# Loads in 2 KB rows, matmul turns, permuted units and new slots in a recurrence-plus-maxout kernel

## Chip, cores, metric

The kernel runs on one core of a Trainium2 chip. The metric is the device time of one execution in microseconds. A profiled execution took some 1.75 us more than the span that its trace shows (402.07 over 400.3). Ratios are computed from fast runs alone: the mean time of one kernel's fast runs over that of the other's in the same rounds, so they are not quite the ratio of the medians quoted.

## The reference

Inputs are float32: x and f_logit of 4 x 6144 x 256, a bound per channel, and three weight matrices.

```python
sig = 1.0 / (1.0 + np.exp(-f_logit))
f = lower_bound + (1.0 - lower_bound) * sig
h = 0
for t in range(S):                       # per batch and channel
    h = f[:, t] * h + (1.0 - f[:, t]) * x[:, t]
    y[:, t] = h
h1, h2 = y @ w1, y @ w2                  # 24576 tokens, 256 -> 1024
out = np.maximum(h1, h2) @ w_out         # 1024 -> 256, float32
```

## The kernel before

The kernel writes max(h1, h2) as h1 + relu(h2 - h1). The engines are called PE (TensorE), ACT (ScalarE), DVE (VectorE), POOL (GpSimd) and SP (SyncE, which issues DMAs). A block of 512 tokens needs "hidden" matmuls with the difference w2 - w1, relus, and a projection with w_out plus a linear part, w1 @ w_out, that is computed once. There are 48 blocks. The scan needs channels on partitions, so tokens must be turned (transposed). Blocks 0 to 3 (the opening) are loaded in float32 and turned on TensorE. Later blocks go in chunks of two through a casting DMA to a scratch tensor and a transposing DMA. The opening's work is a list of items (`PLAN`): G gate (u = sigmoid(-f_logit)), V drive (v = u x), TU and TV turns of u and v, F forget (f from u), S scan, RW rounding of w1 to bf16, D difference of weights, SC its scaling, TW turn of w1, KW its copy, W linear weights, H hidden, R relu, P projection step, warm idle matmuls that only keep TensorE busy; a letter after the dot names the engine (a ACT, v DVE, p POOL).

```python
def load(j, s, q0, q1, eng=nc.sync):                  # 256 KB, rows of 1 KB
    src = (f_logit, x)[s]
    eng.dma_start(out=ins[j][s][:, q0:q1, :],
        in_=src[0, j*TB + q0*P : j*TB + q1*P, :].rearrange("(q p) d -> p q d", p=P))

def turn_pe(j, s, x):
    dst = (uT, vT)[s][j, x] = ps_d.tile([P, KC, HB], BF16, name="dT")   # in PSUM
    src = (us, vs)[s][j]
    for q in range(2):
        for h in range(KC):
            nc.tensor.transpose(dst[:, h, q*P:(q+1)*P],
                                src[:, 2*x+q, h*P:(h+1)*P], ident_b[:])
# [...]
w1n = wpool.tile([P, KC, DFF], FP32)                  # all of w1, four loads of 256 KB
# [...]
def round_w1(k, eng):                                 # one quarter, after its load
    cols = slice(k*QF, (k+1)*QF)
    cast_on(eng, w1b[:, :, cols], w1n[:, :, cols])
# [...]
def diff(k, h, eng):
    cols = slice(k*QF, (k+1)*QF)
    eng.tensor_tensor(out=wdf[:, h, cols], in0=w2n[:, h, cols],
                      in1=w1n[:, h, cols], op=ALU.subtract)
# [...]
for j in range(3, NBLK + 1):                          # the steady loop
    for fc in range(FC):                              # a slot: 0.978 us
        if j < NBLK:
            hidden(j, fc)                             # two 128x512 matmuls and a relu on ACT
        project(j - 1, fc)                            # five 128x256 matmuls
        # [...] stores
        if (j, fc) in gate_of: ...                    # gate, drive, forget, scan of a later block
        if (j, fc) in turn_of: ...                    # transposing DMA of a chunk, cast of the next
```

## Time and profile before

| | before |
|---|---|
| median of 3 runs | 401.4 us (400.9 to 403.14) |
| span of the profiled run | 400.3 us |
| first hidden matmul | 10.18 us |
| first matmul of the loop | 36.08 us |
| start of the last projection | 391.91 us |
| 45 blocks at the loop's pace | 351.9 us |

The page's slices say how busy an engine is. The busy time by stretch says where TensorE is not full, and the timeline says what it waits for there. The prediction below shows those lines and the budget that comes out of them.

### The profile page before, as it was taken

What the parts mean: (1) busy time and instruction counts of PE and PEld (TensorE: products, weight loads), DVE (VectorE), ACT (ScalarE), POOL (GpSimd) and SP (SyncE); (2) the same over time, 40 slices, a digit from 0 to 9 for tenths busy, and PEclk for the clock granted to TensorE, in tenths of its full rate; (3) what the DMA queues carried; (4) which work ended last, traced back from release to release, by engine and by line L of the source; (5) the groups of instructions that cost most, each with busy time, mean ns of one, the idle gap of its engine ahead of it and who ended that gap; (6) DMA issues with size and microseconds to landing.
All of it is one profiled execution on the core that took longest, in us unless ns stands there. A gap on an engine that the chain in (4) does not pass through costs nothing.

```text
span 400.3 us, 7223 instructions
## 1 busy us (share of the span) xinstructions
PE 390.6 (98%) x2854; PEld 276.1 (69%) x2854; DVE 251.5 (63%) x365; ACT 273.8 (68%) x452; POOL 42.3 (11%) x83
## 2 busy tenths in 40 slices
PE   8999999999999999999999999999999999999996
PEld 3887677666777677766776677667776777667764
DVE  4976775738576567657755765676576567657622
ACT  5777675766766676677667667766766776676661
POOL 2511010110111010110110110110201101100000
PEclk9999999999999999999999999999999999999999
DMA  8989996989999999999999999998999999895122
GB/s 259 349 213 202 216 212 145 195 192 218 233 219 218 205 181 219 200 192 218 195 189 222 195 200 212 184 234 186 180 213 209 196 223 194 191 215 146 52 99 87
DMA packets 125110, 79.12 MB, mean 198 GB/s; under 512 B 94226, under 2 KB 101652, under 8 KB 125076
## 3 DMA queue, kind: packets, MB, share of 16 engines
q1 hardware_dynamic: 112836, 55.33, 54.4%
q0 software_dynamic: 11968, 23.07, 35.5%
q8 instruction: 22, 0.36, 0.4%
q10 hardware_dynamic: 272, 0.26, 0.2%
q14 instruction: 12, 0.10, 0.1%
HBM read 53.48 MB, written 48.23 MB: 254 GB/s over the span
## 4 chain that ended last, share of the span: by engine, by line
PE 85%; DMA 7%; DVE 4%; ACT 1%; SPq 1%; issue 1%; DVEq 0%; ACTq 0%
PE psO L263 47%; PE dT L243 35%; DVE y L147 2%; DMA fn<-in_f_logit_dram 2%; PE dT L223 2%; DMA won<-in_moe_w_out_dram 1%; DMA w2n<-in_moe_w_dram 1%; DMA fT<-fs 1%; DMA xT<-xs 1%; ACT u L195 1%; DVE v L199 1%; SPq L178 1%; DVE ff L136 1%; PE dT L124 0%; DVE osb L312 0%
## 5 line engine op out<-in xcount | busy, mean ns | idle before, releaser
L238 ACT ACTIVATE rt<-dT 128x512 bf16<-128x512 f32 x379 | 221.9, 596 | 105.9 <-PE dT L243 103.0
L263 PE MATMUL psO<-wob,rt 128*128 128x256 bf16 x1536 | 231.5, 273 | 2.2 <-ACT rt L238 1.7
L263 PEld LDWEIGHTS <-rt 128*128 128x128 bf16 x1536 | 149.9, 98 | 98.1 <-ACT rt L238 2.5
L243 PE MATMUL dT<-y,wd 128*128 128x512 bf16 x720 | 214.3, 379 | 0.9 <-DVE y L147 0.9
L147 DVE TENSOR_TENSOR_SCAN y<-ff,y,v 128x512 bf16<-128x512 bf16 x82 | 105.3, 1284 | 2.9
L199 DVE TENSOR_TENSOR v<-u,xT 128x1024 bf16<-128x1024 bf16 x44 | 30.4, 692 | 102.3 <-ACT u L195 86.6
L312 DVE COPY osb<-psO 128x512 f32<-128x512 f32 x92 | 62.1, 679 | 28.6 <-PE psO L263 28.6
L243 PEld LDWEIGHTS <-wd 128*128 128x128 bf16 x720 | 70.5, 98 | 8.2
L263 PE MATMUL psO<-w,y 128*128 128x256 bf16 x384 | 72.6, 273 | 0.0
L195 ACT ACTIVATE u<-fT 128x1024 bf16<-128x1024 bf16 x44 | 46.2, 1049 | 4.2 <-DMA fT<-fs 4.2
L184 POOL CAST held<-fT 128x1 f32<-128x1 bf16 x21 | 10.1, 479 | 288.6 <-DMA fT<-fs 288.6
L263 PEld LDWEIGHTS <-y 128*128 128x128 bf16 x384 | 37.5, 98 | 4.4
L136 DVE TENSOR_SCALAR ff<-u,nom 128x512 bf16<-128x512 bf16 x88 | 29.8, 338 | 0.0
L223 PE MATMUL dT<-y,wd 128*128 128x256 bf16 x96 | 14.7, 273 | 0.0
L168 POOL DMA_DIRECT2D fs<-in_f_logit_dram x22 | 12.3, 558 | 2.8 <-issue 2.6
L168 POOL DMA_DIRECT2D xs<-in_x_dram x22 | 12.1, 550 | 0.0
L147 DVE TENSOR_TENSOR_SCAN y<-nff,y,dT 128x256 bf16<-128x256 bf16 x14 | 9.7, 734 | 2.1 <-PE dT L124 1.8
L223 PEld LDWEIGHTS <-wd 128*128 128x128 bf16 x96 | 9.1, 98 | 1.4 <-issue 0.2
L111 DVE TENSOR_TENSOR vn<-un,xn 128x512 bf16<-128x512 bf16 x8 | 6.0, 755 | 5.2 <-ACT un L106 3.3
L428 PE MATMUL psO<-warm 128*128 128x512 bf16 x21 | 7.6, 494 | 1.2 <-DVE warm L556 1.2
L106 ACT ACTIVATE un<-fn 128x512 bf16<-128x512 f32 x8 | 5.0, 628 | 4.5 <-DMA fn<-in_f_logit_dram 4.5
L147 DVE TENSOR_TENSOR_SCAN y<-ff,v 128x512 bf16<-128x512 bf16 x6 | 7.3, 1225 | 0.2
(41 smaller groups left out, 54.7 us busy)
## 6 DMA issues: line engine op xcount, KB each, us to landing
out_dram<-osb SPq DMA_DIRECT2D x95, 256.0 KB, 2.8
fs<-in_f_logit_dram POOLq DMA_DIRECT2D x22, 512.0 KB, 6.1
xs<-in_x_dram POOLq DMA_DIRECT2D x22, 512.0 KB, 9.1
fn<-in_f_logit_dram SPq DMA_DIRECT2D x8, 256.0 KB, 7.3
xn<-in_x_dram SPq DMA_DIRECT2D x7, 256.0 KB, 6.7
w1n<-in_moe_w_dram SPq DMA_DIRECT2D x4, 256.0 KB, 5.4
w2n<-in_moe_w_dram SPq DMA_DIRECT2D x4, 256.0 KB, 5.6
won<-in_moe_w_out_dram SPq DMA_DIRECT2D x4, 256.0 KB, 6.0
```

The costliest lines, as they stand in the source:

```text
L136: nc.vector.tensor_scalar(out=o, in0=i, scalar1=nom[:, h : h + 1], scalar2=1.0, op0=ALU.mult, op1=ALU.add)
L147: nc.vector.tensor_tensor_scan(out=ys[j][:, h, t0:t1], data0=ffs[j][:, h, t0:t1], data1=v, initial=initial, op0=ALU.mult, op1=ALU.add,)
L168: nc.gpsimd.dma_start(out=spare[c % NS, name][:], in_=src[b, k * TB : (k + CB) * TB, :], max_dma_last_dim=4096,)
L184: nc.gpsimd.tensor_copy(out=held[:], in_=turned[c, 0][:, KC - 1, last : last + 1])
L195: nc.scalar.activation(out=us[j][:], in_=part(j, 0), func=AF.Sigmoid, scale=-1.0)
L199: nc.vector.tensor_tensor(out=vs[j][:], in0=us[j][:], in1=part(j, 1), op=ALU.mult)
L223: nc.tensor.matmul(dts[j, fc][:, tok], lhsT=wd[:, kc, unit(fc)], rhs=ys[j][:, kc, tok], start=(first and kc == 0), stop=(not first and kc ...
L238: nc.scalar.activation(out=rt[:], in_=dts[j, fc][:], func=AF.Relu)
L243: nc.tensor.matmul(dts[j, fc][:], lhsT=wd[:, kc, unit(fc)], rhs=ys[j][:, kc, :], start=(kc == 0), stop=(kc == KC - 1),)
L263: nc.tensor.matmul(ps, lhsT=lhsT, rhs=rhs, start=start, stop=stop, skip_group_check=True)
L312: nc.vector.tensor_copy(out=osbs[j, g][:], in_=pos[j, g, 0][:])
L428: nc.tensor.matmul(idle[:].rearrange("p r d -> p (r d)"), lhsT=warm[:, 0:P], rhs=warm[:], start=True, stop=True,)
```

## The change

The intent: larger DMA rows for quicker loads, with the turns adapted to the new layout; an order of the opening made for the new loads; and loop slots that turn chunks and gate blocks earlier, so that no gate waits on a late chunk.

```diff
-        in_=src[0, j*TB + q0*P : ...].rearrange("(q p) d -> p q d", p=P)
+        in_=src[0, t0 : t0 + HB, :].rearrange("(p r) d -> p r d", r=2)     # two tokens a partition

-        dst = ps_d.tile([P, KC, HB], BF16, name="dT")
-                nc.tensor.transpose(dst[:, h, q*P:(q+1)*P], src[...], ident_b[:])
+        dst = ps_d.tile([P, KC, HB], FP32, name="dT")
+                nc.tensor.matmul(dst[:, h, r:HB:2], lhsT=src[...], rhs=ident_b[:], ...)

-            in_=moe_w_out[...].rearrange("(q p) c -> p q c", p=P)
+            in_=moe_w_out[...].rearrange("(p r) c -> p r c", r=2)           # permutes the units

-        cast_on(eng, w1b[:, :, cols], w1n[:, :, cols])
+        cast_on(eng, w1b[:, :, cols].rearrange("p h (r n) -> p h r n", r=2),
+                     w1n[:, :, cols].rearrange("p h (n r) -> p h r n", r=2))
 # [...] scale(): the same stepped view of wdf

-    f0a x0a f0b w13 w23 x0b w12 w22 wo3 w11 w21 w10 wo2 w20 f1a x1a wo1 f1b wo0 x1b
+    f0a x0a f0b x0b w1h w2h f1a wo0 w12 wo1 w22 w13 w23 x1a f1b wo2 x1b wo3 f2a f2b
 # [...] w1h, w2h: the first halves in one load each; PLAN in another order; every load but the
 # bound's on SP's queue (two x loads were on ACT's); hidden matmuls of block 2's end not in halves

-    turn_of = {(4, 1): 1, (6, 0): 2}
-    turn_of |= {(NP + c*CB - 3, 5): c for c in range(3, NCH)}
-    gate_of = {(3, 3): 4, (4, 0): 5, (5, 0): 6, (5, 5): 7, (6, 6): 8, (7, 3): 9}
+    turn_of = {(3, 5): 1, (5, 2): 2, (7, 0): 3}
+    turn_of |= {divmod(FC*(NP + c*CB - 3) - 3, FC): c for c in range(4, NCH)}
+    gate_of = {(3, 1): 4, (3, 6): 5, (4, 5): 6, (5, 3): 7, (6, 3): 8, (7, 1): 9}
 # [...] later gates one slot earlier; eight output buffers in place of six
```

More of the change, by code (lines that the diff above doesn't have):

```diff
@@ L60 @@
     rpool = ctx.enter_context(tc.tile_pool(name="rpool", bufs=3 * FC))
-    opool = ctx.enter_context(tc.tile_pool(name="opool", bufs=6))
+    opool = ctx.enter_context(tc.tile_pool(name="opool", bufs=8))
     lastpool = ctx.enter_context(tc.tile_pool(name="last", bufs=2))
@@ L94, in alloc_in, with load @@
         ys[j] = ypool.tile([P, KC, TB], BF16, name="y")
-    def load(j, s, q0, q1, eng=nc.sync):
+    def load(j, s, half):
         src = (f_logit, x)[s]
-        eng.dma_start(
-            out=ins[j][s][:, q0:q1, :],
-            in_=src[0, j * TB + q0 * P : j * TB + q1 * P, :].rearrange(
-                "(q p) d -> p q d", p=P
-            ),
+        t0 = j * TB + half * HB
+        nc.sync.dma_start(
+            out=ins[j][s][:, 2 * half : 2 * half + 2, :],
+            in_=src[0, t0 : t0 + HB, :].rearrange("(p r) d -> p r d", r=2),
         )
@@ L118, in turn_pe @@
     def turn_pe(j, s, x):
-        dst = (uT, vT)[s][j, x] = ps_d.tile([P, KC, HB], BF16, name="dT")
+        dst = (uT, vT)[s][j, x] = ps_d.tile([P, KC, HB], FP32, name="dT")
         src = (us, vs)[s][j]
-        for q in range(2):
+        for r in range(2):
             for h in range(KC):
-                nc.tensor.transpose(
-                    dst[:, h, q * P : (q + 1) * P],
-                    src[:, 2 * x + q, h * P : (h + 1) * P],
-                    ident_b[:],
+                nc.tensor.matmul(
+                    dst[:, h, r:HB:2],
+                    lhsT=src[:, 2 * x + r, h * P : (h + 1) * P],
+                    rhs=ident_b[:],
+                    start=(r == 0 and h == 0),
+                    stop=(r == 1 and h == KC - 1),
+                    skip_group_check=True,
                 )
@@ L238, in relu, with hidden_whole @@
             nc.scalar.activation(out=rt[:], in_=dts[j, fc][:], func=AF.Relu)
-    def hidden(j, fc):
+    def hidden_whole(j, fc):
         dts[j, fc] = ps_d.tile([P, TB], FP32, name="dT")
@@ L249, in hidden @@
             )
+    def hidden(j, fc):
+        hidden_whole(j, fc)
         relu(j, fc)
@@ L335, with weight_load @@
     QF = DFF // 4
-    def weight_load(k, w, src):
-        cols = slice(k * QF, (k + 1) * QF)
+    def weight_load(c0, c1, w, src):
         nc.sync.dma_start(
-            out=w[:, :, cols], in_=src[:, cols].rearrange("(h p) f -> p h f", p=P)
+            out=w[:, :, c0:c1], in_=src[:, c0:c1].rearrange("(h p) f -> p h f", p=P)
         )
@@ L345, in wout_load @@
             out=won[:, 2 * k : 2 * k + 2, :],
-            in_=moe_w_out[k * QF : (k + 1) * QF, :].rearrange("(q p) c -> p q c", p=P),
+            in_=moe_w_out[k * QF : (k + 1) * QF, :].rearrange("(p r) c -> p r c", r=2),
         )
@@ L356, in round_w1 @@
         cols = slice(k * QF, (k + 1) * QF)
-        cast_on(eng, w1b[:, :, cols], w1n[:, :, cols])
+        cast_on(
+            eng,
+            w1b[:, :, cols].rearrange("p h (r n) -> p h r n", r=2),
+            w1n[:, :, cols].rearrange("p h (n r) -> p h r n", r=2),
+        )
     pts = {}
@@ L380, in scale @@
         cols = slice(k * QF, (k + 1) * QF)
-        o, i, m = wd[:, h, cols], wdf[:, h, cols], om[:, h : h + 1]
+        o = wd[:, h, cols].rearrange("p (r n) -> p r n", r=2)
+        i = wdf[:, h, cols].rearrange("p (n r) -> p r n", r=2)
+        m = om[:, h : h + 1]
         if on_dve:
@@ L440 @@
     LOADS = """
-    f0a x0a f0b w13 w23 x0b w12 w22 wo3 w11 w21 w10 wo2 w20 f1a x1a wo1 f1b wo0 x1b
-    f2a x3b f3a x2a f2b x2b f3b x3a
+    f0a x0a f0b x0b w1h w2h f1a wo0 w12 wo1 w22 w13 w23 x1a f1b wo2 x1b wo3 f2a f2b
+    x2a x3b x2b f3b x3a f3a
     """
     PLAN = """
-    warm1 keeps_T G0a RW3.p V0a keeps TU0a D30.p F0a1.v G0b warm1 TV0a warm3 TU0b
-    F0a0.a S0a1 F0b0.a warm1 TW3 S0a0 F0b1.a KW3.a V0b SC30.a D31.p RW2.v D20.p
-    warm5 TV0b S0b0 D21.p D11.p S0b1 TW2 KW2.v SC31.a H07a SC21.v H06a RO3.a warm3
@@ L448 @@
-    H07b H06b SC20.a R07.a W133 H05a D10.v H05b R06.a RW0.a H04b SC10.v P071 SC11.v
-    H04a RW1.p P060 P061 R05.v D00.v H02b RO2.p TW0 R04.a H02a R02.a G1a D01.p TW1
-    RO1.p P040 H03b KW0.v KW1.a SC00.v P051 SC01.v H03a V1a R03.a W132 P070 TU1a
-    P041 H01b H00b H01a TV1a G1b F1a1.v H00a P030 P020 P031 R00.a RO0.p W131 TU1b
-    P021 F1a0.v S1a1 W130 R01.a P050 F1b0.a S1a0 G2a P010 KL1.a V1b TV1b KL0.a
-    F1b1.v P000 TU2a H11a H14a H16a S1b1 G3a P001 S1b0 P011 L01 F2a1.a H11b V2a H14b
@@ L454 @@
-    L00 F2a0.v H17a G2b O01.a R14.v TV2a L11 R11.a H16b L10 TU2b S2a0 R16.a G3b P140
-    H17b S2a1 H12a H12b P141 F2b1.v P111 R17.a H13b V2b H13a H15a R12.a F2b0.v H15b
-    TV2b P170 TU3b CA H10b H10a R15.a R13.v P110 F3b1.a TU3a R10.a F3b0.a S2b1 P121
-    P130 S2b0 V3a P151 H21a H21b F3a1.a P161 H26b H26a R21.a TV3a P100 V3b H24a
-    F3a0.v R26.a P131 S3a1 H24b H27b P171 H22b TV3b R24.a H27a P101 O00.a S3a0 S3b1
-    P150 R27.a H22a P160 H23a R22.a S3b0 H25b H25a H20b H23b H20a R25.a R23.v R20.v
@@ L460 @@
-    P120 O11.v O10.a
+    G0a RW0.p warm1 keeps_T TU0a keeps V0a F0a1.v D00.p D10.p warm2 TV0a G0b S0a1
+    warm3 TU0b V0b F0a0.a F0b0.a F0b1.a RW1.a S0a0 warm2 TV0b D11.p S0b1 warm3 TW0
+    RW2.p TW1 D01.v KW0.a SC00.a G1a SC01.v warm6 H00a S0b0 RO0.v H01a SC10.v H00b
+    TU1a R00.a SC11.v D21.p H01b KW1.a W130 P001 RW3.p H03b P000 D30.p F1a0.v RO1.v
+    R01.a D31.p D20.v H02a H02b H03a W131 TW2 P011 P010 SC21.v F1a1.a SC20.v R02.a
+    KW2.v TW3 H04a H04b RO2.p R03.a SC30.a V1a P021 KW3.v H05b SC31.v P020 G1b P030
@@ new lines @@
+    RO3.p P031 TV1a H05a TU1b R04.a H07a R05.a S1a0 F1b1.a H07b V1b H06b H06a P040
+    CA P041 S1a1 P050 TV1b F1b0.a S1b0 R06.a W132 R07.a H10a G2a H12a P051 W133 H16a
+    S1b1 P061 KL1.v H13a H12b KL0.v H10b H16b P070 V2a R12.v P071 G2b R10.a L01 V2b
+    TU2a H15b H13b P121 F2a0.v H15a R16.a TU2b TV2a O01.a R13.a F2b1.a L10 H11a
+    R15.a F2b0.a F2a1.v P100 S2a1 L11 TV2b H17a G3a P130 S2a0 H11b P161 S2b0 H17b
+    S2b1 H14b TU3a P060 H14a R11.a F3a1.v R17.a P150 P110 P120 H24 F3a0.v H21 V3a
@@ L461, with load_item @@
+    G3b P170 R14.a R24.a H23 R21.a TU3b V3b F3b0.a R23.v TV3a P140 H20 TV3b S3a1
+    F3b1.v P131 R20.a H27 P160 L00 H22 R27.a S3a0 P151 H26 H25 O10.a S3b1 R22.a P141
+    P171 P111 P101 S3b0 R26.a O00.v O11.v R25.a
     """
     engines = {"a": nc.scalar, "v": nc.vector, "p": nc.gpsimd}
-    def load_item(name, eng=nc.sync):
-        if name[0] == "w":
-            k = int(name[2])
-            if name[1] == "o":
-                wout_load(k)
-            elif name[1] == "1":
-                weight_load(k, w1n, moe_w1)
-            else:
-                weight_load(k, w2n, moe_w2)
-        else:
-            half = 2 * "ab".index(name[2])
-            load(int(name[1]), "fx".index(name[0]), half, half + 2, eng)
+    def load_item(name):
+        if name[:2] == "wo":
+            wout_load(int(name[2]))
+        elif name[0] == "w":
+            w, src = ((w1n, moe_w1), (w2n, moe_w2))[int(name[1]) - 1]
+            k = name[2]
+            weight_load(*((0, HF) if k == "h" else (int(k) * QF, (int(k) + 1) * QF)), w, src)
+        else:
+            load(int(name[1]), "fx".index(name[0]), "ab".index(name[2]))
@@ L523, in issue @@
         elif kind == "H":
-            hidden_half(*arg)
+            (hidden_half if len(arg) == 3 else hidden_whole)(*arg)
         elif kind == "R":
@@ L535, in issue @@
         elif kind == "CA":
-            nc.gpsimd.tensor_copy(out=held[:], in_=ins[2][0][:, 3, D - 1 : D])
+            nc.gpsimd.tensor_copy(out=held[:], in_=ins[2][1][:, 3, D - 1 : D])
             cast(0)
@@ L541, in issue @@
             raise ValueError(item)
-    turn_of = {(4, 1): 1, (6, 0): 2}
-    turn_of |= {(NP + c * CB - 3, 5): c for c in range(3, NCH)}
-    gate_of = {(3, 3): 4, (4, 0): 5, (5, 0): 6, (5, 5): 7, (6, 6): 8, (7, 3): 9}
-    gate_of |= {(b - 2, 5): b for b in range(10, NBLK)}
+    turn_of = {(3, 5): 1, (5, 2): 2, (7, 0): 3}
+    turn_of |= {divmod(FC * (NP + c * CB - 3) - 3, FC): c for c in range(4, NCH)}
+    gate_of = {(3, 1): 4, (3, 6): 5, (4, 5): 6, (5, 3): 7, (6, 3): 8, (7, 1): 9}
+    gate_of |= {(b - 2, 4): b for b in range(10, NBLK)}
     with tc.manual_schedule():
@@ L551 @@
             alloc_in(j)
-        for k, name in enumerate(LOADS.split()):
-            load_item(name, nc.scalar if k in (1, 3) else nc.sync)
-            if k == 0:
-                nc.sync.dma_start(out=lbr[:], in_=lower_bound.rearrange("(h p) -> h p", p=P))
+        nc.scalar.dma_start(out=lbr[:], in_=lower_bound.rearrange("(h p) -> h p", p=P))
+        for name in LOADS.split():
+            load_item(name)
         nc.vector.memset(warm[:], 0.0)
```

## The prediction

> **What bounds the kernel now.** I read the 40 slices first, then the busy time by stretch, then the timeline of PE where a stretch was not full, then the DMA view. On the page, PE is busy in almost every slice, at full clock:
>
> ```profile
> PE   8999999999999999999999999999999999999996
> PEclk9999999999999999999999999999999999999999
> ```
>
> A busy PE is not always a PE at its pace, so I split the span at the first hidden matmul (10.18 us), at the first matmul of the steady loop (36.08), at 100, and at the start of the last projection (about 392). Columns: busy time of PE, PEld, DVE, ACT, POOL with counts, clock, DMA share, GB/s.
>
> ```profile
> 10.18:36.08 25.90, 25.07 (x255) 22.03 (x253) 21.14 (x40) 20.05 (x38) 7.05 (x12) 1.00 1.03 255
> 36.08:100.00 63.92, 60.84 (x431) 41.73 (x429) 40.93 (x58) 42.78 (x70) 4.91 (x11) 1.00 0.93 199
> 100.00:392.00 292.00, 292.00 (x2094) 204.69 (x2092) 182.59 (x254) 205.64 (x335) 27.26 (x51) 1.00 0.91 193
> ```
>
> From 100 to 392 PE never idles. In its timeline a loop slot (two 128x512 hidden matmuls, five 128x256 projections) starts every 0.978 us, so a block of eight slots takes 7.82 us. The loop runs 45 such blocks: 45 x 7.82 = 351.9. The first loop matmul starts at 36.08 and the last projection at 391.91, which is 355.83; so the loop holds 355.83 - 351.9 = 3.9 us of gaps. Distances between hidden starts place them all before 90 us: 0.68 (at 36.7), 1.05 (at 44.6), 1.16 (at 70.1) and 1.03 (at 86.9), sum 3.92. The budget of the span is therefore
>
> 36.08 (opening) + 3.93 (gaps) + 351.9 (loop pace) + 8.39 (last projection, copy, store) = 400.3.
>
> Only the first two terms can be moved by this change. The second and third gap, in the timeline:
>
> ```profile
> 42.96 1.28 DVE L147 TENSOR_TENSOR_SCAN y<-ff,y,v 128x512 bf16<-128x512 bf16 x1
> 44.52 1.28 DVE L147 TENSOR_TENSOR_SCAN y<-ff,y,v 128x512 bf16<-128x512 bf16 x1
> 45.86 0.38 PE L243 MATMUL dT<-y,wd 128*128 128x512 bf16 x1 [0.90 <-DVE y L147]
> ...
> 70.28 1.06 ACT L195 ACTIVATE u<-fT 128x1024 bf16<-128x1024 bf16 x1 [1.91 <-DMA fT<-fs]
> 71.25 2.20 ACT L238 ACTIVATE rt<-dT 128x512 bf16<-128x512 f32 x4
> 71.88 0.28 PE L263 MATMUL psO<-wob,rt 128*128 128x256 bf16 x1 [0.99 <-ACT rt L238]
> ```
>
> In the first, the hidden matmuls of block 4 wait for its scans, whose gate was placed too late in the loop. In the second (and at 86.5 alike), the gate sits at the head of ACT, in order, waiting for a turned chunk to land; the relus behind it are held, and PE runs out of them.
>
> The opening is bound by loads. Columns: packets, MB, share of 16 engines' time.
>
> ```profile
> q1 hardware_dynamic: 5352, 5.16, 107.1%
> ```
>
> That is 5 to 20 us: the engines are full, at 345 GB/s. Loads of 256 KB land about 0.755 us apart: the first at 4.24 us (its gate starts then), the 21st, f2a, at 20.93, where PE waits for it:
>
> ```profile
> 21.61 0.40 PE L124 MATMUL dT<-ident_b,un 128*128 128x128 bf16 x4 [0.82 <-ACT un L106]
> ...
> 23.98 0.19 POOL L536 COPY held<-fn 128x1 f32<-128x1 f32 x1 [5.29 <-DMA fn<-in_f_logit_dram]
> ```
>
> The second line is the trigger for the first chunk's cast, which waits for the 25th load.
>
> **What the Trainium skill says.** (1) "DMA: Bandwidth & Descriptors", section Why small descriptors are slow: each packet has a fixed overhead. The trace agrees in kind. Loads with 1 KB rows: 15 us x 16 x 1.071 / 5352 = 48.0 ns a packet. The window 385 to 400 holds stores with 2 KB rows (512 packets), two of 1 KB rows (256) and 96 tiny ones, 864 packets in 24.2% of 16 engines: 58.1 us in all. Less 256 x 48 ns, that leaves 89 ns or less a 2 KB packet, against 2 x 48 = 96. So a gain of some 8%, for stores; none of the loads before has 2 KB rows. (2) "PSUM — Partial Sum Buffer", section Specifications (TRN2), says of its 8-byte cachelines: "any non-contiguous AP slows matmuls significantly". The new turns write every other f32 column, so this bears on them; no trace of before shows it. (3) "TensorE: Matmul & The Clock Gate", section Back-to-back issue gap: N/2.4 + 2.5 ns warm, 109 ns at N = 256. The trace agrees: eight projections span 0.87 us, and the last 40 take 4.37. (4) "VectorE: DVE Perf Modes", section Why PSUM operands drop a tier: f32 from PSUM runs at the slowest rate. The DVE forgets (348 ns from bf16 PSUM) may grow a little; the scans (about 690 ns for 256 tokens) take about 2.5 ns an element from SBUF as well (1284 ns for 512) and should not.
>
> **The change part by part.**
> (a) 2 KB rows. 6.3 of the 7.3 MB take 2 KB rows (all of x, f_logit, w_out and half of w1, w2). At 89 ns for 2 KB a 256 KB unit takes about 0.70 us instead of 0.755. All 28 units: 24 x 0.055 = 1.3 us saved at the end of the loads, 1.1 at the 21st and 25th.
> (b) Turns. 64 transposes become 64 matmuls of the same 128 columns; the before kernel spaces them 55 ns. No time, if the strided write costs nothing. The output fills a whole bank instead of half, but the pool has five tiles either way.
> (c) Unit permutation: copies with a step of two elements, all off PE; no data moves that did not move before.
> (d) New opening order. Useful PE work ahead of the loop, from the paces above: three hidden blocks 3 x 32 x 0.109 = 10.5, two projections 8.7, 64 turns 3.6, 16 weight turns 0.9, 16 combined-weight matmuls 1.75: 25.4 us. In both kernels 24 of the 128-column turns (1.3 us) come before the first hidden matmul, so 24.1 follow it. Before: 10.18 + 24.1 = 34.3, so 1.8 us was lost until 36.08 (three warm-ups 0.65, the f2a wait 0.82, and crumbs). After: the first hidden matmul needs the halves of w1 and w2, units 5 to 8. The eighth lands at 4.24 + 7 x 0.70 = 9.1; difference on POOL 0.72, scaling on ACT 0.5: first hidden at about 10.4, no sooner than before. From there no warm-up is left in the plan; f2a is again the 21st unit but lands 1.1 us sooner, and walking the plan item by item with durations of before I find each operand ready before PE wants it, within tenths. I allow 0.7 us of losses: loop at 10.4 + 24.1 + 0.7 = 35.2, that is 0.9 earlier.
> (e) New loop slots. The cast's trigger is again the 25th unit, so it comes 1.1 us sooner or more (about 22.8). Chunk 0's f lands turned about 11.8 us after the trigger (24.0 to 35.8 before), so at 34.6, its x about 38. Gate 4 moves from slot (3,3) to (3,1), 2 us sooner in the loop: if its drive starts at 38 its scans end by 42 (0.69 + two times 1.55), and hidden 4 starts at 35.2 + 7.8 = 43. The 1.05 gap closes. Gate 6 moves up by three slots, but the turn it waits for goes from (4,1) to (3,5), four slots, and the casts behind run ahead. Its f should land near 47 (cast 35.1, 6 to 8 us to land, 4.7 to turn), the gate comes at 35.2 + 13.7 = 48.9. Gates 8 and 10 get more room: in the steady part turn and gate are 15 slots apart, 14.7 us, against 8 before. I expect both of these gaps gone, and leave 0.6 us for crumbs there and at the loop's entry, where the last scans of block 3 are tight.
> Sum: 35.2 + 0.6 + 351.9 + 8.4 = 396.1 of span. The median run time of before is 1.1 over its profiled span, so 397.2; I say 397.
>
> **The rivals.** (R1) Strided PSUM writes slow the turns: doubling would cost 64 x 55 ns = 3.5 us of PE, about 2 beyond idle time: 399. For: the skill's sentence. Against: the written column pitch is 8 bytes only, and many turns stand near waits. (R2) The new order starves the opening: all weights of units 0 to 3 must come before any hidden matmul, and a late w2 moves everything by as much; 1 us late gives 398. For: loads bind until 20 us. (R3) The gate still blocks ACT, since turns are placed earlier than casts can land, and then SP holds the stores too: the two gaps of 1.1 us return, 399. For: cast, landing and turn of a chunk need some 11 us and DMA is near full in the loop. Against: 15.6 us is the period. (R4) Everything fits and the opening loses nothing, first hidden at 10: 394.5 + 0.6.
>
> **Range and chances.** Perfect overlap, 34.1 + 351.9 + 8.4 + 1.1 = 395.5, is the floor unless the first hidden matmul comes much sooner; two rivals at once give about 400.5. Range 394.5 to 400. Over 2% faster needs 393.4, under that floor: 5%. Over 2% slower needs a fault I don't see: 3%.
>
> **What would show it.** Right: the loop's first hidden matmul near 35, PE gaps between 36 and 100 together under 1 us, packets of the opening near 85 to 90 ns for 2 KB, turn pace still 55 ns, slot pace 0.978. Wrong: turns spaced 100 ns or more (R1); a first hidden matmul after 11 (R2); "PE waits for rt" with a gate ahead on ACT (R3); a first hidden matmul before 9.5 would make me too slow.

## The result

The changed kernel took 407.34 us (median of 4 runs, 406.31 to 408.53) against 401.35 before; ratio 1.0142, 95% interval 1.0099 to 1.0184. It is slower by 1.4%, and outside the predicted range.

The page of the changed kernel, its 40 slices of 10.2 us: busy tenths of TensorE, its granted clock, busy tenths of the DMA engines.

```profile
PE   7399999999999999999999999999999999999996
PEclk9599999999999999999999999999999999999999
DMA  7989349999999999999999899999999999991122
```

The second slice is new: TensorE nearly idle and then at half its clock. Busy time by stretch (columns as in the prediction):

```profile
10.00:15.00 5.00, 0.00 (x0) 0.00 (x0) 1.75 (x4) 0.00 (x0) 0.00 (x0) 0.63 1.08 370
15.50:20.00 4.50, 3.65 (x16) 1.94 (x17) 1.45 (x2) 2.17 (x4) 4.34 (x7) 0.50 1.04 381
...
47.21:100.00 52.79, 52.42 (x374) 36.99 (x379) 35.04 (x49) 37.65 (x61) 3.82 (x9) 1.00 0.93 192
```

For five microseconds TensorE, ACT and POOL do nothing, while the DMA engines are full. The last row is the loop from its first matmul, at 47.21: here the trace lacks five matmul records (374 beside 379 weight loads), and the list of waits has no TensorE wait; so the loop has no gap left. The last projection starts at 399.11, which is 47.21 + 351.9. So the opening lost 11.1 us, the loop won its 3.9, and the rest (the end after the last projection) is 0.7 shorter: +6.5 of span. The waits, as total, times, longest, name the culprit:

```profile
POOL w1b L356 <- DMA w1n<-in_moe_w_dram: 14.4, 1, 14.4
PE dT L403 <- POOL w1b L356: 7.2, 1, 7.2
```

And the timeline around it:

```profile
15.66 0.63 POOL L356 CAST w1b<-w1n 128x512 bf16<-128x512 f32 x1 [14.36 <-DMA w1n<-in_moe_w_dram]
16.26 2.08 POOL L385 TENSOR_TENSOR wdf<-w2n,w1n 128x256 f32<-128x256 f32 x3
16.35 1.03 PE L403 MATMUL dT<-ident_b,w1b 128*128 128x128 bf16 x8 [7.21 <-POOL w1b L356]
17.17 2.77 PE L440 MATMUL psO<-warm 128*128 128x512 bf16 x6
19.73 1.49 PE L226 MATMUL dT<-y,wd 128*128 128x256 bf16 x6
```

POOL's first rounding of w1 waits until 15.66 for loads. The differences of the weights stand behind it on POOL, in order, and every hidden matmul needs those. Yet the half of w2 had landed by 11.32, when DVE took it. What did the rounding wait for? The listing of the built program answers, without a run. In the built program the DMAs that SP and ACT issue signal on eight semaphores in turn, so a number can be traced to its load (the listing is shortened):

```
before   POOL  w1b <- w1n   [waits DMA 4]            its own load
changed  POOL  w1b <- w1n   [waits DMA 5, 4, 1]      w1h, w13 and w12: all three loads of w1
         POOL  wdf <- w2n   [waits DMA 6]            w2h alone
```

The rounding reads only the first quarter, which w1h brings. But it reads w1 through a stepped view of four dimensions. Over its two halves of the contraction, the range from the view's first to last address covers columns of w12 and w13 too. My reading is that the dependence tracker takes that whole range as read; no run shows how it decides. The range alone is not enough: the unstepped view of the kernel before spans as much, and its first rounding started at 6.33, when the later loads of w1 were still on their way. So the step, or the fourth dimension that it brings, is part of the cause. That the wait is false, and what it costs, the experiments show.

The turns also differ. Before, four turns took 0.22 us of TensorE's time, from one start to the next:

```profile
18.87 0.39 PE L124 MATMUL dT<-ident_b,un 128*128 128x128 bf16 x4
19.09 0.38 PE L263 MATMUL psO<-wob,rt 128*128 128x256 bf16 x2
```

In the changed kernel they take 0.40:

```profile
26.51 0.60 PE L124 MATMUL dT<-ident_b,vn 128*128 128x128 bf16 x4
26.91 0.42 PE L226 MATMUL dT<-y,wd 128*128 128x256 bf16 x2
```

### The profile page after: what moved, and what is told of

It reads as the page before. It is cut to its first block, busy times and chain, and to the rows that moved or that the text cites. A ratio compares the mean times of both kernels' runs of the same rounds, so it can differ in the third digit from the quotient of the medians.

```text
span 406.8 us, 7152 instructions
## 1 busy us (share of the span) xinstructions
PE 392.8 (97%) x2795; PEld 279.3 (69%) x2841; DVE 252.4 (62%) x366; ACT 273.5 (67%) x451; POOL 36.8 (9%) x83
## 4 chain that ended last, share of the span: by engine, by line
PE 95%; DMA 2%; SPq 2%; issue 1%; POOL 0%; DVE 0%; POOLq 0%
PE psO L269 52%; PE dT L246 38%; DMA w1n<-in_moe_w_dram 2%; PE dT L226 2%; PE dT L124 1%; PE psO L440 1%; SPq L344 1%; SPq L100 1%; SPq L350 0%; PE psO L420 0%; PE dT L403 0%; POOL w1b L356 0%; DVE row L333 0%; POOLq L356 0%
## 5 line engine op out<-in xcount | busy, mean ns | idle before, releaser
L246 PE MATMUL dT<-y,wd 128*128 128x512 bf16 x690 | 208.8, 379 | 2.2
L187 POOL CAST held<-fT 128x1 f32<-128x1 bf16 x21 | 4.4, 211 | 291.7 <-DMA fT<-fs 291.7
L226 PE MATMUL dT<-y,wd 128*128 128x256 bf16 x64 | 10.8, 290 | 0.0
L440 PE MATMUL psO<-warm 128*128 128x512 bf16 x24 | 9.2, 529 | 1.2 <-DVE warm L563 1.2
L403 PE MATMUL dT<-ident_b,w1b 128*128 128x128 bf16 x16 | 1.8, 265 | 7.2 <-POOL w1b L356 7.2
L403 PEld LDWEIGHTS <-w1b 128*128 128x128 bf16 x16 | 1.4, 119 | 7.7 <-POOL w1b L356 7.7
```

Source lines behind the costliest of these rows:

```text
L187: nc.gpsimd.tensor_copy(out=held[:], in_=turned[c, 0][:, KC - 1, last : last + 1])
L226: nc.tensor.matmul(dts[j, fc][:, tok], lhsT=wd[:, kc, unit(fc)], rhs=ys[j][:, kc, tok], start=(first and kc == 0), stop=(not first and kc ...
L246: nc.tensor.matmul(dts[j, fc][:], lhsT=wd[:, kc, unit(fc)], rhs=ys[j][:, kc, :], start=(kc == 0), stop=(kc == KC - 1),)
L440: nc.tensor.matmul(idle[:].rearrange("p r d -> p (r d)"), lhsT=warm[:, 0:P], rhs=warm[:], start=True, stop=True,)
```

## The experiments

Theory: the false wait makes most of the opening's loss, the turns a smaller part, and the loop slots are a plain gain. Rivals: the large weight loads are themselves late; the halved clock is the cost; the loop's gaps closed only because the loop started late. "Loop start" below is the first hidden matmul of block 3 in the trace.

| run | time, us | ratio to before, 95% | loop start, us |
|---|---|---|---|
| changed kernel | 407.34 | 1.0142 (1.0099 to 1.0184) | 47.21 |
| e1_own_tiles | 401.39 | 0.9997 (0.9972 to 1.0022) | 39.79 |
| e2_perm_alone | 408.63 | 1.0177 (1.0154 to 1.0201) | 42.56 |
| e3_slots_alone | 398.78 | 0.9931 (0.9900 to 0.9963) | 36.06 |
| e4_rows_turns | 403.61 | 1.0049 (1.0023 to 1.0074) | 37.09 |
| e5_own_ucheap | 400.14 | 0.9976 (0.9963 to 0.9988) | 38.60 |
| e6_slots_perm_own | 398.01 | 0.9922 (0.9909 to 0.9936) | 35.29 |
| e7_quarters | 400.53 | 0.9988 (0.9976 to 1.0001) | 38.50 |
| e8_after_warm (misbuilt) | 408.21 | 1.0169 (1.0143 to 1.0195) | 46.62 |
| e9_own_1k | 398.82 | 0.9943 (0.9931 to 0.9956) | 37.28 |
| e10_best | 398.00 | 0.9922 (0.9907 to 0.9937) | 36.11 |
| e11_warm_filled | 406.04 | 1.0100 (1.0081 to 1.0118) | 44.50 |
| e12_plain_writes (wrong result) | 399.03 | 0.9947 (0.9933 to 0.9961) | 37.73 |

All but e12 were correct. Each is quoted against the kernel before as run in its own rounds.

### The false wait taken away

```diff
-    w1n = wpool.tile([P, KC, DFF], FP32)
+    w1h  = wpool.tile([P, KC, DFF // 2], FP32)
+    w12  = wpool.tile([P, KC, DFF // 4], FP32)
+    w13q = wpool.tile([P, KC, DFF // 4], FP32)      # each load its own buffer; same instructions
```

> The changed kernel, with w1's three loads landing in three buffers of their own in place of one, so that the roundings of w1 no longer wait for loads they don't read. Theory (false waits): in the changed kernel the first rounding on POOL waited for three loads until 15.7 us, and with it the differences, the first hidden matmul (19.7) and the whole opening. Without it the first hidden matmul should start when the first half of w2 has landed (11.3) plus 1.2: about 12.5, the loop about 39 to 40 in place of 47.2, no TensorE idle near 7 us and no clock at half: some 400 to 401 us in all, level with the kernel before. Rival (the half-sized weight loads are what is late): the loop starts above 44 still, 405 or more. My prediction's view, that nothing else is wrong: 397.

The first rounding now waits for one load. Its timeline:

```profile
9.26 0.64 POOL L361 CAST w1b<-w1h 128x512 bf16<-128x512 f32 x1 [7.95 <-DMA w1h<-in_moe_w_dram]
10.64 2.32 POOL L390 TENSOR_TENSOR wdf<-w2n,w1h 128x256 f32<-128x256 f32 x3 [0.74 <-DMA w2n<-in_moe_w_dram]
...
11.99 0.28 PE L228 MATMUL dT<-y,wd 128*128 128x256 bf16 x1
12.45 1.03 PE L228 MATMUL dT<-y,wd 128*128 128x256 bf16 x5 [0.17 <-DVE wd L403]
```

The rounding starts at 9.26 in place of 15.66, the first hidden matmul at 11.99 in place of 19.73, the loop 7.4 us sooner, at full clock throughout. By the run times the false wait cost 6.0 us (407.34 against 401.39), or 6.8 by the repetition of the changed kernel (408.21, e8 below). The theory holds. It also confirms that the wait was false: the same instructions ran sooner and the result was correct. The time is level with before, not 397, so other parts of the opening still cost something.

### The permutation alone, with its wait

```diff
 # kernel before, plus:
+    stepped views in round_w1() and scale(); w_out loaded "(p r) c -> p r c"
```

> The kernel before, with the unit permutation alone: strided rounding and scaling of w1 and wd, w_out in 2 KB rows; same order, same turns, same slots. Theory (false waits): the first rounding now waits for all four loads of w1, the last landing near 13 us in place of 6.3, so the first hidden matmul moves from 10.2 to about 16 to 17, TensorE idles more than 3 us and is granted half its clock for some us: 405 to 409 us. Rival (the permutation costs nothing, or only the strided copies do): 401 to 402.

The first rounding in the kernel before:

```profile
6.33 0.61 POOL L350 CAST w1b<-w1n 128x512 bf16<-128x512 f32 x1 [5.03 <-DMA w1n<-in_moe_w_dram]
```

and with the permutation, with the turn of w1 that waits for it:

```profile
13.05 0.87 POOL L350 CAST w1b<-w1n 128x512 bf16<-128x512 f32 x1 [11.75 <-DMA w1n<-in_moe_w_dram]
...
13.98 0.61 PE L397 MATMUL dT<-ident_b,w1b 128*128 128x128 bf16 x4 [6.96 <-POOL w1b L350]
```

In the untouched order, the same stepped view alone moves the first rounding from 6.33 to 13.05 and costs 7.1 us. That is more than the whole change lost, 6.0.

### The slots alone, then with the permutation and no false wait

```diff
 # e3: kernel before, plus the new turn_of, gate_of and eight output buffers
 # e6: e3, plus the permutation of e2, and:
-    w1n = wpool.tile([P, KC, DFF], FP32)
+    w1q = [wpool.tile([P, KC, DFF // 4], FP32, name=f"w1q{k}") for k in range(4)]
```

> The kernel before, with the other turn and gate slots of the loop and eight output buffers alone. Theory: the three gaps of 1.05, 1.16 and 1.03 us between 44 and 89 us close, as they did in the changed kernel: 398 us (3.2 less). Rival (they closed there only because a loop that started 11 us later found its chunks landed; with the loop at 36 the gates block ACT as before): 400 to 401.5.

> e3_slots_alone with the unit permutation of e2_perm_alone on top (strided rounding and scaling, w_out in 2 KB rows), but w1's quarters in four buffers of their own. Theory (in e2 the false wait was all of the 7 us; strided copies cost nothing that shows): 398.8 us as e3, within 0.7. Rival (the permutation itself costs): 401 or more.

The loop of e3 up to 100, to be set beside the row of before from 36.08 to 100 in the prediction (60.84 busy of 63.92):

```profile
36.06:100.00 63.94, 62.84 (x447) 44.18 (x453) 43.25 (x62) 45.66 (x75) 6.71 (x14) 1.00 1.09 222
```

The loop starts when it did before, the last projection starts 3.26 us sooner, and of TensorE's waits in the loop only the 0.7 at its entry is left. So the slots are worth the three later gaps whatever the start of the loop; the rival falls. By the run times they are worth 2.7 us (398.78 against 401.52): the profiled execution of the kernel before, 402.07, was 0.7 above its median. In e6 the permutation costs nothing any more: 398.01, its interval overlapping that of e3.

### The turns

```diff
 # e4: kernel before, f_logit and x in 2 KB rows, turns as in the changed kernel
 # e5: e1, but u turned by transposes into plain runs; the forget step reads two runs
 # e9: e1, but 1 KB rows and transposes for all, as before
 # e12: e1, but (wrong on purpose: token order)
-                    dst[:, h, r:HB:2],
+                    dst[:, h, r * P : (r + 1) * P],
```

> The kernel before, with f_logit and x loaded in 2 KB rows and turned by matmuls that write every other f32 column; all else as before. Theory: a turn takes 98 ns in place of 55 as in the changed kernel's trace, 48 of the 64 lie after the first hidden matmul: 2.1 us more on TensorE, less up to 0.8 from quicker loads: 402 to 403.5. Rival (turns hide in waits): 401; if the loads were the bound and gained more than the turns cost: 400.

> e1_own_tiles with the turns of u (half of the 64) as contiguous transposes again, the forget steps reading two runs of 128 in place of one of 256; v still turned by matmuls that write every other column. Theory (each strided turn costs 43 ns more on TensorE, and after the first hidden matmul TensorE is the bound): 24 of these 32 lie there, so the loop starts 1.0 us sooner, 38.7: 400.3 us against 401.4. Rival (turns hide in waits): no change, 401.4.

> e1_own_tiles with f_logit and x in 1 KB rows and all turns as transposes, as before the change. Theory: 48 turns after the first hidden matmul are 43 ns cheaper, 2.1 us less; the loads are slower by 8% and take some of it back, 0.3 us at the first hidden matmul: 399.5 us against 401.4. Rival (loads bind this opening, so the slower rows cost more than the turns give): 402.

> e1_own_tiles with the turning matmuls writing two plain runs of 128 columns in place of every other column; nothing else. Wrong on purpose: the tokens of a pair of rows come out in another order. Theory (the step in the PSUM write is what makes a turn take 99 ns, not that it is a matmul in place of a transpose): a turn takes 55 ns, the loop starts about 2 us sooner than e1's 39.8: 399.4 us against 401.4. Rival (a matmul of 128 columns with f32 output is slower than a transpose whatever it writes): 99 ns still, 401.4.

All four came out within 0.7 us of the theory, and none near its rival: 403.6 (0.1 above the range given), 400.1, 398.8 and 399.0. In e12 the turns are still matmuls with f32 output, and only the step of the write is gone:

```profile
26.61 0.39 PE L126 MATMUL dT<-ident_b,un 128*128 128x128 bf16 x4
26.83 0.39 PE L126 MATMUL dT<-ident_b,vn 128*128 128x128 bf16 x4
27.05 0.60 PE L271 MATMUL psO<-w,y 128*128 128x256 bf16 x4
```

Four turns take 0.22 us again. So it is the stepped write to PSUM (the accumulator memory that TensorE writes), not the matmul, that makes a turn 99 ns instead of 55; the loop starts 2.06 us sooner without it. The plain write can't simply be used for v: the build refuses a scan whose operands are not one flat row, so they must be in token order.

The rows bring what was estimated of them. From 15 to 20 us, the queue of loads before and in e1 (packets, MB, share of 16 engines' time):

```profile
q1 hardware_dynamic: 1785, 1.72, 107.8%
```

```profile
q1 hardware_dynamic: 1044, 1.90, 103.6%
```

That is 48.3 ns a 1 KB packet before, and at most 89.5 ns a 2 KB packet in e1 (118 smaller ones left out of the count), 383 GB/s against 347. But in the new order it bought nothing: e9 has the slow rows and e12 the quick ones, with turns equally cheap, and e9's loop starts 0.45 us sooner (their times agree, 398.82 and 399.03, with overlapping intervals). In the old order the first hidden matmul came 0.64 us sooner with the quick rows (e4, 9.54 against 10.18), and the stepped turns took more than that back: e4's loop starts 1.0 later.

### The order of the weights

```diff
 # e1 with the first halves as quarters, each with its buffer:
-    f0a x0a f0b x0b w1h w2h f1a wo0 ...
+    f0a x0a f0b x0b w10 w20 w11 w21 f1a wo0 ...
```

> e1_own_tiles with the first halves of w1 and w2 loaded as quarters (1 KB rows), first w1 and w2 of units 0 and 1, then those of units 2 and 3, each in its own buffer. Theory (what is left of the late start is that 1 MB of weights must land, at 10.6, before the first difference): the sixth unit lands about 9.2, the first hidden matmul starts near 10.6 in place of 12.0, the loop up to 1.4 sooner: 400 us. Rival (the start is set by something else, or the gain is lost to later waits, since the rest arrives no sooner): 401.4.

Inconclusive in time: 400.53, its interval overlapping that of e1. In the trace the scaled weights of units 0 and 1 are ready at 11.0 in place of 12.4, but the first hidden matmul starts at 11.69, only 0.3 sooner, because the plan puts the turn of the second quarter and six idle matmuls ahead of it. The loop starts 1.3 us sooner, and 0.7 of that is lost again at the end, after the last projection. The early loads do bind, but the plan was not made for that order.

### The clock

```diff
 # changed kernel, false wait kept:
-    ... TV0b D11.p S0b1 warm3 TW0
+    ... TV0b D11.p S0b1 warm9 warm9 warm9 warm6 TW0
```

> The changed kernel with the false wait left in, but 30 more idle matmuls put into the 7.2 us in which TensorE waits for it, so that its clock is not halved. Theory: the first hidden matmul is set by POOL and DVE, 19.2 in place of 19.7, and the matmuls up to about 22 run at full clock: the loop starts about 1 to 1.5 us sooner, 46: 406 us in place of 407.3; the clock is a small part of the loss. Rival (the halved clock is what the idle cost): 403 or less.

> What e8_after_warm was meant to be (its item for 33 idle matmuls was read as 3, so it was the changed kernel unaltered): the false wait left in, and 30 more idle matmuls in the 7.2 us of idle, in four items of 9, 9, 9 and 6. Theory: the first hidden matmul 19.2 in place of 19.7, the matmuls up to about 22 at full clock, the loop 1 to 1.5 us sooner than 47.2: 406 us in place of 407.3; the clock is a small part of the loss. Rival (the halved clock is what the idle cost): 403 or less.

The first attempt was built wrong, as told, and is a repetition of the changed kernel (408.21). The second kept TensorE busy during the wait:

```profile
16.17 1.46 PE L440 MATMUL psO<-warm 128*128 128x512 bf16 x6
17.46 0.82 PE L226 MATMUL dT<-y,wd 128*128 128x256 bf16 x6
```

At full clock the six idle matmuls ahead of the first hidden one take 1.3 us, against 2.56 at half clock, where they held up ready work: the scaling on ACT was done at 18.0, and the hidden matmul started at 19.73. The loop starts at 44.50, 2.7 us sooner than in the changed kernel and 2.1 sooner than in its repetition e8, whose loads landed earlier as e11's did. So the clock's part is some 2 us, more than the 1 to 1.5 I expected, and a minor part of the false wait's 7.4.

### The best version

```diff
 # e6 with
-    R25.a R23.v R20.v
+    R25.a R23.v R20.a
```

> e6_slots_perm_own with one relu of the opening's end (unit 0 of block 2) on ACT in place of DVE, where it stood behind another and TensorE waited 0.73 us for it at the loop's entry. Theory: that gap shrinks to about 0.2: 397.5 us against 398.0. Rival (the copy behind it on ACT then delays a projection's bank): 398.

No gain: 398.00, as e6. The 0.73 us gap at the loop's entry is gone from the list of waits, but in the profiled run another wait, 1.6 us for a drive of an opening block, took its place. Either version is 0.8% faster than before and 2.3% faster than the changed kernel, by the medians.

## Why the prediction was wrong

**What bounds the kernel, and the budget: right.** The loop's pace was the same in every kernel, and all differences lie in the opening, the gaps and 0.7 us at the very end.

**(e), the slots: right.** Foreseen 0.6 us of gaps left; measured none in the changed kernel, 0.7 with the slots alone.

**(c), the permutation: the step that failed.** It said: "copies with a step of two elements, all off PE; no data moves that did not move before." The copies are cheap, as e6 shows. But the stepped view changed what one of them waits for, and that copy stands first on POOL. Step (d) inherited it: "I find each operand ready before PE wants it" took the rounding as ready when w1h had landed. With the false wait and its clock loss the loop starts 7.4 us later than without, at 47.21 (e1 against the changed kernel; 6.0 to 6.8 by the run times); 35.2 was foreseen. The listing of the built program, which shows the waits, was there to be read before any run; I read it for the order of instructions and not for the waits.

**(b) and R1, the turns: sized wrongly.** The prediction made the turns free and R1 a rival: "doubling would cost 64 x 55 ns = 3.5 us of PE, about 2 beyond idle time". Measured: 44 ns a turn, and 2.06 us of loop start. R1 was right, on the sentence of the Trainium skill that the prediction quoted and then set aside.

**(d), the first hidden matmul: mis-sized without the wait too.** Foreseen 10.4; in e1 it is 11.99. The second half of w2 landed at 10.64, not 9.1: I took loads to land in order of issue at an even pace. The prediction's own lines spoke against the pace: from the first load at 4.24 to the 21st at 20.93 is 0.83 us a load, not 0.755. By 10.64 e1 had moved 0.78 MB up to 5 us, 1.58 from 5 to 10 and 0.25 after, 2.6 MB, where the loads up to w2h are 2.1; later loads had taken their share of the engines.

**(a), the rows: size right, use wrong.** A 2 KB packet took some 89 ns, as estimated from the stores. The loop did not start sooner for it. (A slip in the sum: 17 of the first 21 units have the larger rows, so the 21st should gain 0.9 us, not 1.1.)

**R2 and R3.** R2 ("the new order starves the opening") named the right kind of loss, a wait for weights, with the wrong cause; 1.2 us of it is real (e9 against before, with neither false wait nor stepped turns; e9's first hidden matmul is 1.6 us late, at 11.80). R3 did not occur.

The 11.13 us by which the loop started late in the two profiled executions split, by pairs of runs, into 1.20 (order, with the permutation; before to e9), 2.51 (rows and turns; e9 to e1), 4.71 (false wait at full clock; e1 to e11) and 2.71 (half clock; e11 to the changed kernel, some 0.6 of it chance in when the loads landed: the profiled execution was the slowest of four). Each start comes from one profiled execution, so the parts are good to about half a microsecond. **Open:** the end after the last projection is 8.3 to 8.4 us in some kernels and 7.6 to 7.7 in others (the changed kernel and all that were made from it but e7), and no run tells why.

## What to carry to other kernels

When an operand becomes a stepped or reshaped view of a buffer that several loads fill, look at the waits of the built instruction before timing it: a stepped view whose range spans other loads' bytes can wait for all of them, and giving each load its own buffer took that away at no cost in time here. Look first at what stands at the head of an in-order engine, since everything behind it inherits its wait, and at filler matmuls, which slow down with the clock and then delay ready work. And a write that steps through PSUM is paid on TensorE (44 ns in each turn of 128 columns), so a layout that makes loads 10% quicker can still lose where TensorE, not the load, is the bound.

## What the Trainium skill lacked or had wrong

- "PSUM — Partial Sum Buffer", Specifications (TRN2), says that a non-contiguous access pattern slows matmuls significantly, without a number. Here a 128-column matmul that writes every other f32 column takes 99 ns in place of 55 (e1 against e12).
- "Perfetto Trace Analysis", Transposes, advises transposes over standard matmuls for turning. Here an identity matmul of bf16 with plain f32 writes keeps the same 55 ns pace as the transpose (e12 against before); only the step in the write cost time.
- "DMA: Bandwidth & Descriptors", Where 436 GB/s comes from, says that about 358 GB/s binds transfers between HBM and SBUF. With this kernel on one core, loads in 2 KB rows moved 383 GB/s here (e1, 15 to 20 us), and 347 in 1 KB rows. The same page's table of measured loads goes higher for one core, so the sentence is too low as it stands there. The section on small descriptors has no figure for these two sizes: 48 ns and at most 89.5 ns a packet.
- No page that I found tells that a stepped view of a tile can add waits for loads that it doesn't read: in this kernel 7.4 us at the start of the loop and 6.0 of the run time (e1), in the kernel before 7.1 of the run time (e2).
- "TensorE: Matmul & The Clock Gate", HAM oscillation, says that a long wait without matmuls brings the clock down to half. The runs agree: after 7.2 us the granted clock was 0.50. It doesn't warn of idle matmuls placed ahead of ready work to hold the clock; these are slowed like the others: six took 2.56 us in place of 1.3.
